# One PSUM layout for the spectral part and the attention loop, and the first scores between the last spectral products

## The chip, the core and the metric

The kernel runs on one core of a Trainium2 chip. The core has a matrix engine (TensorE, PE in the profile; its weight loads are shown apart as PEld), VectorE (DVE), ScalarE (ACT), GpSimd (POOL) and the DMA queues, the main one of which is issued from SyncE (SP). TensorE writes its results to PSUM, which here is used as eight banks of 128 x 512 float32 values. VectorE and ScalarE read PSUM; GpSimd works only on SBUF in this kernel. The metric is device time in microseconds of one execution; lower is better.

## What is computed

The input is x with 2048 rows of 512 values. The output mixes full multi-head attention (32 heads of 16 values) with a Fourier mixing layer, by a gate for each row:

```python
qkv = (x @ wqkv)                                   # 2048 x 1536
q, k, v = split_heads(qkv)                         # 32 heads of 16
p = softmax(einsum("qd,kd->qk", q, k) / 4)         # 2048 x 2048 for each head
a = concat_heads(p @ v) @ wo
re, im = x_b @ dft_hid_re.T, x_b @ dft_hid_im.T    # 2048 x 512
b = dft_seq_re @ re - dft_seq_im @ im              # the spectral part
g = sigmoid((x * gate_w).sum(-1))
out = g * a + (1 - g) * b
```

All is float32. The kernel feeds TensorE with pairs (hi, lo) of rounded values where it needs the precision: a product of two matrices is then three products, hi x hi, hi x lo and lo x hi.

## The kernel before, in words

The softmax subtracts a maximum for each query, so the kernel first *scans*: TensorE computes scores with queries on the partitions, and VectorE takes their maximum. The maxima then enter the real scores as two more rows of the operands (`m_d`, the hi and lo of the negated maximum), so that ScalarE can evacuate a score tile with one exponential. A scan is one pair of matmuls, for two heads at once; there are 1024 of them (`TOTAL`), of which the first 692 (`FRONT`) are put between the matmuls of the earlier parts, and the rest into the attention loop.

The parts stand in this order:

1. Projections of q, k, v, and the hidden transform of the spectral part (lines 317 to 526).
2. The spectral products (lines 528 to 604): 96 units `n` of a coefficient block (`coef`), four units (u = 0 to 3) to an output tile of 128 rows `t`. A unit covers four of the 16 sequence blocks `s`. Each block is three products, each product two matmuls that use one half of the rows of TensorE each (`halves_of`). The output tile lies in one two-bank PSUM tile, `xy`, of which there are two that take turns. `beside()` after each product puts a folded scan in where its pace says so: such a scan uses one of four single banks, d0, d1, k0, k1; ScalarE evacuates one half of the keys (`fold`, line 153) and VectorE folds the other half into it with the maximum (line 155). `prepare` (line 307) has GpSimd split the coefficients of unit n + 3 into hi and lo, in two rings of four tiles. A finished tile is evacuated in two halves, `tx` on ScalarE (line 598) and, for the last tile, `ty` on VectorE (line 600).
3. The attention loop (lines 893 to 936): 512 steps, for 16 pairs of heads p, two halves h of the queries and 16 blocks kb of keys. A step computes the scores of two heads and two query groups c of 512. Group c = 0 goes to a two-bank tile (`bank2`, the tag s3) and one wide exponential into `eb` (line 649); group c = 1 goes to two single banks (`bank`, the tag s2, three of them) and two narrow exponentials into `e` (line 653), the second one (j = 1) first. Between the two groups stands a scan (`next_scan`, line 130) in another two-bank tile (`pair_banks`, the tag s1). At the end of a step the sums of the step before are added up in `pvb` (`pv`, line 660): four column groups of TensorE, one for each head and query group. Step 0 has no sums. From step 333 (`MIX`) on the last spectral tiles and the output projection fill the place of the scans.

The order of the work is the order in which the source issues it (`manual_schedule`); every engine runs its own instructions in that order, and semaphores hold an instruction until its operands are there and its tile is free. Before, the PSUM pools of the spectral part (`psf`, `psk`) end before the pool of the loop (`ps2`) begins, so the first tiles of the loop take over banks from tiles of other names and shapes.

Of the kernel before, what the change touches and what calls it, by code (L numbers as in the profile page):

```python
# [25 lines left out]
ND = D // P  # L26
NC = S // 512
VC = DH + 1
SCALE = DH ** -0.5
# [6 lines left out]
FRONT = 564 + 16 * LATER  # L36
# [5 lines left out]
MIX = TOTAL - FRONT + 1  # L42
OUT = MIX + NB * LATER
SLOW = 3


def build(tc, x, xT, wqkv, wo, wrT, wiT, cr, ci, gate, out):
    nc = tc.nc
    with ExitStack() as ctx:
        keep = ctx.enter_context(tc.tile_pool(name="keep", bufs=1))  # L50
        stk = ctx.enter_context(tc.tile_pool(name="stk", bufs=6))
        sm = ctx.enter_context(tc.tile_pool(name="sm", bufs=2))
        big = ctx.enter_context(tc.tile_pool(name="big", bufs=1, reuse_waits="tile"))
        dram = ctx.enter_context(tc.tile_pool(name="dram", bufs=1, space=DRAM))

        q_d = [dram.tile([P, 2, S], F32, name=f"q_d{f}") for f in range(ND)]
        k_d = [dram.tile([P, 2, S], F32, name=f"k_d{f}") for f in range(ND)]
# [24 lines left out]
        scanned, used, unfolded = {}, {}, {}  # L82
# [99 lines left out]
        def block(i):  # L182
            return big.tile([P, 512], F32R, tag=f"b{i}", name=f"b{i}")

        ah, al = {}, {}


        seen, slots, due, count = [0], [0], [], [0]
        pace = [None, 0.0]
        with ExitStack() as pf:  # L190
            psf = pf.enter_context(tc.tile_pool(name="psf", bufs=2, space=PSUM))
            cw = pf.enter_context(tc.tile_pool(name="cw", bufs=4, reuse_waits="tile"))

            def s1():
                return pss1[0].tile([P, 2, 512], F32, tag="s1", name="s1")
# [56 lines left out]
            beds = []  # L252
# [41 lines left out]
            coef = []  # L294
# [4 lines left out]
            coef = coef[:len(coef) - NU * LATER]  # L299
# [7 lines left out]
            def prepare(n, copy=nc.gpsimd.tensor_copy, sub=nc.gpsimd.tensor_sub):  # L307
                if n >= len(coef):
                    return
                hi, lo = (cw.tile([P, 512], F32R, tag=tag, name=tag + "_").rearrange("p (c q) -> p c q", q=P)  # L310
                          for tag in ("chi", "clo"))
                raw = craw.pop(n)
                copy(hi, raw)
                sub(lo, raw, hi.bitcast(F32))
                ready[n] = hi, lo

            with ExitStack() as px:
# [11 lines left out]

                def new_cw():  # L330

                    return [[cw.tile([P, 512], F32R, tag=tag, name=tag + "_") for d in range(ND)]
                            for tag in ("chi", "clo")]

                def split_w(w, d, raw, engine=nc.vector, cols=slice(0, 512)):
                    split(w[0][d][:, cols], w[1][d][:, cols], raw[:, cols], engine)
# [188 lines left out]
                    project_s(wi, t, -1.0, use)  # L525
                run_due(True)

            with ExitStack() as py:
# [5 lines left out]
                psk = py.enter_context(tc.tile_pool(name="psk", bufs=1, space=PSUM, reuse_waits="tile"))  # L534
                beds += [lambda tag: psk.tile([P, 512], F32, tag=tag, name="s"), cp]
                for n in range(4, 8):
                    fetch(n)
                for d in range(4):
# [3 lines left out]
                pss, yre, early = {}, {}, {}  # L542
# [8 lines left out]
                for n, (ph, t, u) in enumerate(coef):  # L551
# [11 lines left out]
                    hi, lo = ready.pop(n)  # L563
# [21 lines left out]
                    for w in range(CS):  # L585
                        s = u * CS + w
                        for i, (c_, a_) in enumerate(((hi, ah[s]), (hi, al[s]), (lo, ah[s]))):
                            halves_of(pss[t], c_[:, w, :], a_, s == 0 and i == 0, s == NB - 1 and i == 2)
                            beside()
                        if swap:  # L590
                            if s == 7:
                                for i in range(8, 11):
                                    early[i] = load_operand(1, i, cp)
                            after(1 + 3 * (s % 8), renew, s)
                    if u == NU - 1:
                        tx = cp.tile([P, D], F32, tag="tx", name="tx")
                        ty = cp.tile([P, D], F32, tag="ty", name="ty")
                        nc.scalar.mul(tx, pss[t][0], gm[:, t:t + 1])
                        if n == len(coef) - 1:
                            nc.vector.tensor_scalar_mul(ty, pss[t][1], gm[:, t:t + 1])  # L600
# [5 lines left out]
        assert seen[0] == FRONT, seen[0]  # L606

        with ExitStack() as pa:
            ps2 = pa.enter_context(tc.tile_pool(name="ps2", bufs=1, space=PSUM, reuse_waits="tile"))
# [4 lines left out]
            pvb = ps2.tile([P, 512], F32, tag="pv", name="pvb")  # L614
            nc.vector.memset(pvb, 0.0)
            rb = ap.tile([P, 512], F32, name="rb")
            nc.gpsimd.memset(rb, 1.0)


            both = [pr.tile([P, 2, 512], F32, name=f"eb{i}") for i in range(4)]  # L620
            single = [[pr.tile([P, 512], F32, name=f"e{j}_{i}") for i in range(3 + j)] for j in range(2)]
            turn = [0, 0]

            def pair_banks():
                return ps2.tile([P, 2, 512], F32, tag="s1", name="s1")

            def bank():
                return ps2.tile([P, 512], F32, tag="s2", name="s2", bufs=3)

            def bank2():  # L630
                ps = ps2.tile([P, 2, 512], F32, tag="s3", name="s3")
                return ps, (ps[:, 0, :], ps[:, 1, :])

            def qk2(p, h, kb, c):
                n = turn[c]
                turn[c] += 1
                q0 = h * 1024 + c * 512
                qs, ks = used[p]
                if c == 0:
                    ps, pss = bank2()  # L640
                else:
                    pss = [bank() for j in range(2)]
                for j in range(2):
                    b = 64 * j
                    nc.tensor.matmul(pss[j], ks[b:b + 50, kb * P:(kb + 1) * P],  # L645
                                     qs[b:b + 50, q0:q0 + 512], start=True, stop=True)
                if c == 0:
                    e = both[n % len(both)]
                    nc.scalar.activation(e, ps, AF.Exp, scale=SCALE)  # L649
                    return [e[:, j, :] for j in range(2)]  # L650
# [5 lines left out]
            quads = [(c, j, 64 * c + 32 * j) for c in range(2) for j in range(2)]  # L656

            def pv(p, h, kb, es):
                for c, j, r in quads:
                    nc.tensor.matmul(pvb[r:r + VC, :], va[:, kb, 2 * p + j, :], es[c][j],  # L660
                                     start=kb == 0, stop=kb == NB - 1, tile_position=(0, r))

            def quotients(p, h):
                ob = ap.tile([P, 512], F32, tag="ob", name="ob", bufs=2)
# [193 lines left out]
            groups = {}  # L858

            def part(t, *ks):  # L860

                if t not in groups:
                    if t in (3, 8):
                        ps = pair_banks()
                        groups[t] = ps[:, 0, :], ps[:, 1, :]
                    else:
                        groups[t] = bank2()[1] if t == 9 else (bank(), pvb if t == 11 else bank())
                for k in ks:
                    mix_rest(t, groups[t], k, k == 0 or 7 < t < 11, k == 2)

# [22 lines left out]
            for step in range(NP * PERIODS):  # L893
                p, i = step // PERIODS, step % PERIODS
# [14 lines left out]
                        load_y(c + 2 * (step > OUT))  # L909
                if step >= MIX and step % 2 == 0:  # L910
                    next(fill)
                es = [qk2(p, h, kb, 0)]
                if step == 0:
                    es.append(qk2(p, h, kb, 1))
                if late:
                    late.pop(0)()
                next_scan()
                if step:
                    es.append(qk2(p, h, kb, 1))
                if step >= MIX and step % 2:  # L920
                    next(fill)
# [87 lines left out]
```

## Time and profile before

| | us |
|---|---|
| median of 3 runs | 1755.81 (1754.96 to 1759.93) |
| the profiled execution | 1751.4 |
| its span | 1749.6 |
| TensorE busy in the span | 1719.9 |
| ScalarE busy | 1451.9 |
| VectorE busy | 1155.1 |
| GpSimd busy | 712.7 |

The page adds up busy time over the whole span. Matmuls overlap, so a busy TensorE is not one at its peak. Times within the span are counted from its start. In the chain of work that ended last, each row is a stretch of one engine and line with its start and length; "issue" is time in which nothing that the profile shows was waited for. In the timeline a row gives start, length, engine, line, operation and tiles, and in brackets the idle time before it with what ended it. In a table by stretch a row gives the stretch, its length, the busy time (and count) of PE, PEld, DVE, ACT and POOL, then the clock granted to TensorE as a share of the full one, the share of the DMA engines and GB/s.

### The profile page before, as it was taken

What the parts mean: (1) busy time and instruction counts of PE and PEld (TensorE: products, weight loads), DVE (VectorE), ACT (ScalarE), POOL (GpSimd) and SP (SyncE); (2) the same over time, 40 slices, a digit from 0 to 9 for tenths busy, and PEclk for the clock granted to TensorE, in tenths of its full rate; (3) what the DMA queues carried; (4) which work ended last, traced back from release to release, by engine and by line L of the source; (5) the groups of instructions that cost most, each with busy time, mean ns of one, the idle gap of its engine ahead of it and who ended that gap; (6) DMA issues with size and microseconds to landing.
All of it is one profiled execution on the core that took longest, in us unless ns stands there. A gap on an engine that the chain in (4) does not pass through costs nothing.

```text
span 1749.6 us, 35589 instructions
## 1 busy us (share of the span) xinstructions
PE 1719.9 (98%) x13640; PEld 1021.8 (58%) x13640; DVE 1155.1 (66%) x1876; ACT 1451.9 (83%) x2384; POOL 712.7 (41%) x814
## 2 busy tenths in 40 slices
PE   8999999999999999999999999999999999999998
PEld 6887787888888887333333333333334555555554
DVE  6799999999999887666666666666664212222333
ACT  5445346888887887999999999999999888888885
POOL 3678667555556664032322323232232322322222
PEclk9999999999999999999999999999999999999999
DMA  8782666434354445433232423515313254255612
GB/s 296 254 298 79 190 201 206 121 115 117 104 154 140 139 133 120 74 59 63 58 67 56 82 40 64 95 23 99 78 35 73 64 118 90 68 141 137 177 36 100
DMA packets 126810, 199.55 MB, mean 114 GB/s; under 512 B 54016, under 2 KB 56560, under 8 KB 119728
## 3 DMA queue, kind: packets, MB, share of 16 engines
q1 hardware_dynamic: 84368, 161.02, 34.4%
q0 software_dynamic: 38496, 19.47, 5.2%
q10 hardware_dynamic: 3776, 16.78, 3.6%
q8 instruction: 107, 1.75, 0.4%
q14 instruction: 63, 0.52, 0.1%
HBM read 133.04 MB, written 63.71 MB: 112 GB/s over the span
## 4 chain that ended last, share of the span: by engine, by line
PE 89%; DMA 3%; DVE 3%; POOL 2%; issue 2%; ACT 1%; SPq 0%; DVEq 0%; ACTq 0%; POOLq 0%
PE pvb L660 28%; PE xy L180 21%; PE s L645 19%; PE s L180 8%; PE s L149 7%; PE s L130 6%; DVE mx L132 1%; DMA fa<-ks_d 1%; DMA kf_d<-fa 1%; POOL s L215 1%; DMA raws<-wqkv 0%; DMA raws<-xT 0%; POOL el L215 0%; POOL fa L215 0%; DMA abr<-ab_d 0%
## 5 line engine op out<-in xcount | busy, mean ns | idle before, releaser
L132 DVE TENSOR_REDUCE mx<-s 128x2 f32<-128x1024 f32 x524 | 627.2, 1222 | 207.5 <-PE s L130 207.4
L649 ACT ACTIVATE eb<-s 128x1024 f32<-128x1024 f32 x512 | 579.3, 1131 | 55.1 <-PE s L645 55.1
L653 ACT ACTIVATE e<-s 128x512 f32<-128x512 f32 x1024 | 610.3, 708 | 0.4 <-PE s L645 0.4
L660 PE MATMUL pvb<-e,va 128*17 128x512 f32 x2048 | 517.3, 598 | 0.0
L660 PE MATMUL pvb<-eb,va 128*17 128x512 f32 x2048 | 517.1, 598 | 0.0
L645 PE MATMUL s<-qs,ks 50*128 50x512 f32 x2048 | 428.1, 438 | 2.3 <-DVE ty L600 1.6
L645 PEld LDWEIGHTS s<-qs,ks 50*128 50x128 f32 x2048 | 212.6, 185 | 372.4 <-ACT eb L649 282.6
L155 DVE CUSTOM_DVE_ANT_0 fold<-s,fold 128x512 f32<-128x512 f32 x500 | 339.1, 690 | 39.0 <-PE s L149 19.4
L153 ACT ACTIVATE fold<-s 128x512 f32<-128x512 f32 x500 | 296.1, 602 | 70.0 <-PE s L149 43.1
L149 PE MATMUL s<-ks,qs 48*128 48x512 f32 x1000 | 223.3, 404 | 7.6 <-DVE mx L155 6.1
L130 PE MATMUL s<-ks,qs 48*128 48x512 f32 x1048 | 221.6, 396 | 3.7 <-DVE mx L132 2.5
L668 POOL DMA_DIRECT2D lc<-ob x124 | 63.1, 515 | 308.2 <-DVE ob L665 307.9
L660 PEld LDWEIGHTS pvb<-eb,va 128*17 128x17 f32 x2048 | 69.2, 96 | 190.2 <-issue 182.0
L149 PEld LDWEIGHTS s<-ks,qs 48*128 48x128 f32 x1000 | 120.9, 184 | 47.6 <-DVE mx L155 18.2
L675 POOL DMA_DIRECT2D r_d<-lc x31 | 18.1, 585 | 294.9 <-DVE lc L674 286.0
L130 PEld LDWEIGHTS s<-ks,qs 48*128 48x128 f32 x1048 | 108.3, 184 | 14.9 <-DVE mx L132 6.0
L180 PE MATMUL xy<-w,b 64*128 64x512 f32 x768 | 105.2, 392 | 0.2 <-ACT s L379 0.2
L401 ACT ACTIVATE tx<-xy 128x512 f32<-128x512 f32 x48 | 28.7, 599 | 78.6 <-PE xy L180 52.5
L754 DVE SCALAR_TENSOR_TENSOR y<-s,g,y 128x512 f32<-128x512 f32 x50 | 36.6, 748 | 76.6 <-PE s L180 76.0
L677 POOL DMA_DIRECT2D rb<-r_d x124 | 60.6, 496 | 63.0 <-DMA r_d<-lc 63.0
L180 PE MATMUL s<-b,chi 64*128 64x512 f32 x542 | 85.2, 390 | 0.3 <-ACT chi L963 0.3
L180 PEld LDWEIGHTS xy<-w,b 64*128 64x128 f32 x768 | 72.5, 186 | 17.6 <-ACT s L379 1.0
(750 smaller groups left out, 2320.4 us busy)
## 6 DMA issues: line engine op xcount, KB each, us to landing
craw<-ci SPq DMA_DIRECT2D x64, 256.0 KB
craw<-cr SPq DMA_DIRECT2D x60, 256.0 KB
ks<-k_d SPq DMA_DIRECT2D x46, 256.0 KB
qs<-q_d SPq DMA_DIRECT2D x46, 256.0 KB
ab_d<-ab SPq DMA_DIRECT2D x32, 256.0 KB
y_d<-y SPq DMA_DIRECT2D x32, 256.0 KB
o_d<-oh POOLq DMA_DIRECT2D x28, 256.0 KB, 9.8
o_d<-ol POOLq DMA_DIRECT2D x28, 256.0 KB, 11.9
```

The source lines that it names most:

```text
L130: nc.tensor.matmul(ps[:, j, :], qs[b:b + 48, qb * P:(qb + 1) * P], ks[b:b + 48, c * 512:(c + 1) * 512], start=True, stop=True)
L132: nc.vector.tensor_reduce(mx[p][:, :, qb, c], ps, axis=AX.X, op=ALU.max)
L149: nc.tensor.matmul(ps, qs[b:b + 48, qb * P:(qb + 1) * P], ks[b:b + 48, c * 512:(c + 1) * 512], start=True, stop=True)
L153: nc.scalar.activation(fold[j], ps, AF.Relu)
L155: nc.vector.tensor_tensor_reduce(out=fold[j], in0=ps, in1=fold[j], scale=1.0, scalar=-3.0e38, op0=ALU.add, op1=ALU.max, accum_out=mx[p][:, ...
L180: nc.tensor.matmul(ps[j], lhs[r], rhs[r], start=first, stop=last)
L645: nc.tensor.matmul(pss[j], ks[b:b + 50, kb * P:(kb + 1) * P], qs[b:b + 50, q0:q0 + 512], start=True, stop=True)
L649: nc.scalar.activation(e, ps, AF.Exp, scale=SCALE)
L653: nc.scalar.activation(e[j], pss[j], AF.Exp, scale=SCALE)
L660: nc.tensor.matmul(pvb[r:r + VC, :], va[:, kb, 2 * p + j, :], es[c][j], start=kb == 0, stop=kb == NB - 1, tile_position=(0, r))
L668: nc.gpsimd.dma_start(lc[32 * n:32 * n + 32, :], ob[r + DH:r + VC, :].rearrange("p (s e) -> p s e", e=16))
L677: nc.gpsimd.dma_start(rb[r:r + DH, :], r_d[p][h][n:n + 1, :].to_broadcast([DH, 512]))
```

## The change

1. *PSUM.* One pool, `psf`, now holds two two-bank tiles, `wide0` and `wide1`, for the whole kernel, and `psk` the four single banks d0, d1, k0, k1 from the spectral part on. In the spectral part the two wide tiles take turns as `xy`; in the loop `wide0` serves the scans (s1) and `wide1` the first scores (s3); d0, d1, k0 are the single banks of the second scores, taken in the order of their last use (`order_`), and k1 holds the sums `pvb`.
2. *The first scores.* `qk_both` computes one score pair into `wide1` with its exponential. It is called three times in the last two units of the last spectral tile of part 2, behind the blocks s = 9, 11 and 14: both query groups of step 0 (both by a wide tile and a wide exponential now), and the first group of step 1. `pvb` is cleared at the first call.
3. *The loop's start.* Step 0 issues nothing but the note that its exponentials exist (`continue`), so it has no scan either; step 1 begins with the sums of step 0 and then issues its second group only. All later scans stand one step later.
4. *SBUF.* The hi and lo of a coefficient block lie in one tile of 128 x 2 x 512 of a ring of four (`ring4`); the wide exponentials `eb` take over the same ring. The last `ty` uses another ring's tile.

```diff
+SCANS_IN = 0
+AHEAD = (9, 11, 14)
...
+        ring4 = ctx.enter_context(tc.tile_pool(name="ring4", bufs=4, reuse_waits="tile"))
+        psf = ctx.enter_context(tc.tile_pool(name="psf", bufs=1, space=PSUM, reuse_waits="tile"))
...
+        def wide(i, name):
+            return psf.tile([P, 2, 512], F32, tag=f"wide{i}", name=name)
+
+        def coefficients():
+            t = ring4.tile([P, 2, 512], F32R, tag="c", name="c")
+            return t[:, 0, :], t[:, 1, :]
...
+        def qk_both(p, h, kb, c=0):
+            ps = wide(1 - SCANS_IN, "s3")
+            qk(p, h, kb, c, [ps[:, j, :] for j in range(2)])
+            if len(both) < 4:
+                both.append(ring4.tile([P, 2, 512], F32, tag="c", name="eb"))
+            e = both[ebs[0] % 4]
+            ebs[0] += 1
+            nc.scalar.activation(e, ps, AF.Exp, scale=SCALE)
+            return [e[:, j, :] for j in range(2)]
...
             def xy():
-                ps = psf.tile([P, 2, 512], F32, tag="xy", name="xy")
+                turns[0] += 1
+                ps = wide(turns[0] % 2, "xy")
...
+            order_ = ["d0", "d1", "k0"]
+
+            def bank():
+                order_.append(order_.pop(0))
+                return narrow(order_[-1], "s2")
...
+                        if n >= len(coef) - 2 and s in AHEAD:
+                            if not ahead:
+                                sums.append(narrow("k1", "pvb"))
+                                nc.vector.memset(sums[0], 0.0)
+                            ahead.append(qk_both(0, 0, int(s == AHEAD[2]), int(s == AHEAD[1])))
...
             def pair_banks():
-                return ps2.tile([P, 2, 512], F32, tag="s1", name="s1")
+                return wide(SCANS_IN, "s1")
...
                 for j in (1, 0):
                     nc.scalar.activation(e[j], pss[j], AF.Exp, scale=SCALE)
+                order_[-2:] = order_[-1], order_[-2]
                 return e
...
-                es = [qk2(p, h, kb, 0)]
                 if step == 0:
+                    pend.append((p, h, kb, ahead[:2]))
+                    continue
+                if step == 1:
+                    flush()
+                es = ahead[2:] if step == 1 else [qk2(p, h, kb, 0)]
+                if step == 1:
                     es.append(qk2(p, h, kb, 1))
                 if late:
                     late.pop(0)()
                 next_scan()
-                if step:
+                if step > 1:
                     es.append(qk2(p, h, kb, 1))
```

More of the change, by code (lines that the diff above doesn't have):

```diff
@@ L183, in block, with qk @@
             return big.tile([P, 512], F32R, tag=f"b{i}", name=f"b{i}")
-        ah, al = {}, {}
+        turns = [0]
+        def wide(i, name):
[3 more added lines that the diff above has]
+            return t[:, 0, :], t[:, 1, :]
+        ah, al = {}, {}
+        quads = [(c, j, 64 * c + 32 * j) for c in range(2) for j in range(2)]
+        both = []
+        def qk(p, h, kb, c, pss):
+            q0 = h * 1024 + c * 512
+            qs, ks = used[p]
+            for j in range(2):
+                b = 64 * j
+                nc.tensor.matmul(pss[j], ks[b:b + 50, kb * P:(kb + 1) * P],
+                                 qs[b:b + 50, q0:q0 + 512], start=True, stop=True)
+        def qk_both(p, h, kb, c=0):
[7 more added lines that the diff above has]
+            return [e[:, j, :] for j in range(2)]
+        ebs, ahead, sums = [0], [], []
         seen, slots, due, count = [0], [0], [], [0]
@@ L190, in build @@
         with ExitStack() as pf:
-            psf = pf.enter_context(tc.tile_pool(name="psf", bufs=2, space=PSUM))
-            cw = pf.enter_context(tc.tile_pool(name="cw", bufs=4, reuse_waits="tile"))
             def s1():
@@ L309, in prepare @@
                     return
-                hi, lo = (cw.tile([P, 512], F32R, tag=tag, name=tag + "_").rearrange("p (c q) -> p c q", q=P)
-                          for tag in ("chi", "clo"))
+                hi, lo = (t.rearrange("p (c q) -> p c q", q=P) for t in coefficients())
                 raw = craw.pop(n)
@@ L330, in new_cw @@
                 def new_cw():
-                    return [[cw.tile([P, 512], F32R, tag=tag, name=tag + "_") for d in range(ND)]
-                            for tag in ("chi", "clo")]
+                    return list(zip(*(coefficients() for d in range(ND))))
                 def split_w(w, d, raw, engine=nc.vector, cols=slice(0, 512)):
@@ L526, in build, with narrow @@
                 run_due(True)
+            psk = ctx.enter_context(tc.tile_pool(name="psk", bufs=1, space=PSUM, reuse_waits="tile"))
+            def narrow(tag, name):
+                return psk.tile([P, 512], F32, tag=tag, name=name)
+            order_ = ["d0", "d1", "k0"]
+            def bank():
+                order_.append(order_.pop(0))
+                return narrow(order_[-1], "s2")
             with ExitStack() as py:
@@ L532, in fetch @@
                         load_coef(n, cp.tile([P, CS, P], F32, tag="craw", name="craw", bufs=5))
-                psk = py.enter_context(tc.tile_pool(name="psk", bufs=1, space=PSUM, reuse_waits="tile"))
-                beds += [lambda tag: psk.tile([P, 512], F32, tag=tag, name="s"), cp]
+                beds += [lambda tag: narrow(tag, "s"), cp]
                 for n in range(4, 8):
@@ L594, in build @@
                             after(1 + 3 * (s % 8), renew, s)
+                        if n >= len(coef) - 2 and s in AHEAD:
+                            if not ahead:
+                                assert seen[0] == FRONT, (seen, n, s, pace)
+                                sums.append(narrow("k1", "pvb"))
+                                nc.vector.memset(sums[0], 0.0)
+                            ahead.append(qk_both(0, 0, int(s == AHEAD[2]), int(s == AHEAD[1])))
                     if u == NU - 1:
                         tx = cp.tile([P, D], F32, tag="tx", name="tx")
-                        ty = cp.tile([P, D], F32, tag="ty", name="ty")
+                        last = n == len(coef) - 1
+                        ty = cp.tile([P, D], F32, tag="raw" if last else "ty", name="ty", bufs=3 if last else 2)
                         nc.scalar.mul(tx, pss[t][0], gm[:, t:t + 1])
-                        if n == len(coef) - 1:
+                        if last:
                             nc.vector.tensor_scalar_mul(ty, pss[t][1], gm[:, t:t + 1])
@@ L604, in build @@
                 run_due(True)
-        assert seen[0] == FRONT, seen[0]
+        assert seen[0] == FRONT and turns[0] % 2 == SCANS_IN, (seen, turns)
         with ExitStack() as pa:
-            ps2 = pa.enter_context(tc.tile_pool(name="ps2", bufs=1, space=PSUM, reuse_waits="tile"))
             pr = pa.enter_context(tc.tile_pool(name="pr", bufs=1, reuse_waits="tile"))
@@ L612, in build @@
             ap = pa.enter_context(tc.tile_pool(name="ap", bufs=1, reuse_waits="tile"))
-            pvb = ps2.tile([P, 512], F32, tag="pv", name="pvb")
-            nc.vector.memset(pvb, 0.0)
+            pvb = sums[0]
             rb = ap.tile([P, 512], F32, name="rb")
             nc.gpsimd.memset(rb, 1.0)
-            both = [pr.tile([P, 2, 512], F32, name=f"eb{i}") for i in range(4)]
             single = [[pr.tile([P, 512], F32, name=f"e{j}_{i}") for i in range(3 + j)] for j in range(2)]
-            turn = [0, 0]
+            turn1 = [0]
             def pair_banks():
-                return ps2.tile([P, 2, 512], F32, tag="s1", name="s1")
[L627 to L632, printed above, removed]
+                return wide(SCANS_IN, "s1")
             def qk2(p, h, kb, c):
[L635 to L638, printed above, removed]
                 if c == 0:
[L640 to L650, printed above, removed]
+                    return qk_both(p, h, kb)
+                n = turn1[0]
+                turn1[0] += 1
+                pss = [bank() for j in range(2)]
+                qk(p, h, kb, c, pss)
                 e = [ring[n % len(ring)] for ring in single]
@@ L653, in qk2 @@
                     nc.scalar.activation(e[j], pss[j], AF.Exp, scale=SCALE)
+                order_[-2:] = order_[-1], order_[-2]
                 return e
-            quads = [(c, j, 64 * c + 32 * j) for c in range(2) for j in range(2)]
             def pv(p, h, kb, es):
@@ L661, in pv, with bank2 @@
                                      start=kb == 0, stop=kb == NB - 1, tile_position=(0, r))
+            def bank2():
+                ps = wide(1 - SCANS_IN, "s3")
+                return ps[:, 0, :], ps[:, 1, :]
             def quotients(p, h):
@@ L866, in part @@
                     else:
-                        groups[t] = bank2()[1] if t == 9 else (bank(), pvb if t == 11 else bank())
+                        groups[t] = bank2() if t == 9 else (bank(), pvb if t == 11 else bank())
                 for k in ks:
```

## The prediction

> **What bounds the kernel now.** I read the page first (span, busy time, chain by engine), then the chain in order of time around the place that the change touches, then the timeline there, and last tables by stretch for the clock.
>
> ```profile
> span 1749.6 us, 35589 instructions
> PE 1719.9 (98%) x13640; PEld 1021.8 (58%) x13640; DVE 1155.1 (66%) x1876; ACT 1451.9 (83%) x2384; POOL 712.7 (41%) x814
> PE 89%; DMA 3%; DVE 3%; POOL 2%; issue 2%; ACT 1%; SPq 0%; DVEq 0%; ACTq 0%; POOLq 0%
> ```
>
> TensorE is busy for 98% of the span and carries 89% of the chain. Time can only be won where TensorE waits or runs slowly. The change touches one such place, the seam between the last spectral product and the attention loop. This is the chain there:
>
> ```profile
> 688.55 0.50 PE s L149
> 689.05 4.35 PE xy L180 x36
> ...
> 693.48 0.70 ACT tx L598
> ...
> 694.20 0.76 DVE ty L600
> ...
> 695.01 0.69 PE s L645 x2
> ...
> 695.78 1.03 ACT eb L649
> ...
> 696.85 0.80 PE s L645 x2
> 697.65 0.61 PE s L130 x2
> 698.26 0.43 PE s L645 x2
> 698.69 1.84 PE pvb L660 x8
> ...
> 703.45 0.43 PE s L645 x2
> 703.88 0.23 PE s L130 x2
> 704.11 0.23 PE s L645 x2
> 704.34 0.98 PE pvb L660 x8
> 705.33 0.43 PE s L645 x2
> ```
>
> The spectral products end at 693.40 (689.05 + 4.35). The first scores wait for both evacuations of the last spectral tile (tx on ScalarE, then ty on VectorE), the second scores wait for the first exponential, and the sums (pvb) of step 0 take 1.84 us where 0.98 is normal later. Step 3 is the first step at the steady pace: it starts at 703.45, and the next one at 705.33, 1.88 us later. So the seam lasts 703.45 - 693.40 = 10.05 us, for three steps of which the first has no sums.
>
> Why 1.84 and not 0.98? Tables by stretch (the busy time of TensorE comes second, the granted clock after the count of POOL):
>
> ```profile
> 545.81:549.22 3.41, 1.81 (x15) 1.32 (x14) 3.41 (x8) 0.97 (x3) 1.23 (x1) 1.00 0.26 78
> 549.22:552.63 3.41, 3.41 (x18) 2.98 (x17) 2.22 (x7) 1.95 (x5) 0.85 (x2) 0.50 0.04 9
> 569.71:573.11 3.40, 1.91 (x17) 1.59 (x18) 1.72 (x5) 2.60 (x5) 1.28 (x1) 1.00 0.78 241
> 573.12:576.53 3.41, 3.41 (x32) 2.75 (x32) 2.70 (x9) 2.30 (x5) 1.91 (x2) 1.00 0.11 40
> 692.58:695.99 3.41, 1.79 (x13) 1.04 (x9) 1.24 (x2) 0.90 (x2) 0.96 (x1) 1.00 0.00 0
> 695.99:702.82 6.83, 6.13 (x25) 1.93 (x28) 3.55 (x3) 5.33 (x9) 2.06 (x3) 0.50 0.64 151
> 702.82:712.00 9.18, 9.18 (x74) 3.29 (x70) 5.37 (x6) 8.55 (x14) 0.00 (x0) 1.00 0.56 89
> ```
>
> The clock was halved from 549.22 to 552.63 and from 695.99 to 702.82: lengths of 3.41 and 6.83 (twice 3.41), and the two starts lie 146.77 = 43 x 3.413 apart. So in this trace the clock is decided on a grid of 3.41 us. It fell after cells in which TensorE was busy for 1.81 and 1.79 us, and stayed after a cell with 1.91. A cell must be idle for about 1.6 us (3.41 - 1.81) to lose the clock; the seam's first gap alone (693.40 to 695.01) does that, if one cell holds it.
>
> The Trainium skill ("TensorE: Matmul & The Clock Gate", Part 1) calls the window free-running, 3413 ns long, which the grid of 3.41 agrees with. It also asks for a whole idle window before the clock falls, and under "Why this matters for your kernels" only forbids gaps above some 3 us; by that rule the seam would cost no clock, before or after. Here the trace disagrees: 1.6 us of idle time was enough, twice.
>
> **The change, part by part.** In the order of the built programs, TensorE has the same instructions in number; SP's and POOL's queues keep their order throughout. Differences stand at the seam alone, and one wide exponential replaces two narrow ones.
>
> *Three score pairs between the last spectral products.* They come after blocks 9, 11 and 14 of the last accumulation, the first right behind the last folded scan (688.55). A pair that finds its operands costs 0.23 (row 704.11), so 3 x 0.23 = 0.69, and the spectral part ends at 694.09. Do they wait? Their loads must have landed, their two banks must be free, and ScalarE must keep up:
>
> ```profile
> 688.39 0.60 ACT L153 ACTIVATE fold<-s 128x512 f32<-128x512 f32 x1 [0.17 <-PE s L149]
> 688.00:690.00 2.00, 1.81 (x16) 1.23 (x14) 1.84 (x6) 0.82 (x2) 0.00 (x0) 1.00 0.04 11
> 690.00:693.40 3.40, 3.38 (x29) 2.50 (x26) 0.00 (x0) 0.00 (x0) 0.00 (x0) 1.00 0.00 0
> 705.26 0.50 PE L645 MATMUL s<-qs,ks 50*128 50x512 f32 x2
> 705.80 1.04 ACT L649 ACTIVATE eb<-s 128x1024 f32<-128x1024 f32 x1
> ```
>
> ScalarE's last fold ends at 688.99, and from 690.00 to 693.40 ScalarE, VectorE and the DMA engines do nothing: the exponentials have a free engine. The loads are all there by 690.00 at the latest (the DMA share before that is 0.04), so pair 1 could wait 1.0 at most. An exponential starts 0.54 after its pair (705.26 to 705.80) and takes 1.03. Pair 1 at about 689.0 gives its banks back at 690.6; six products (1.4 us) lie before pair 2, at 690.65, so it waits for next to nothing. Pair 3 stands nine products (2.1 us) behind that. I take no wait; the bound above is 1.03 for each of the two.
>
> *The two waits that go.* The scores no longer wait for ty (1.61) nor step 1's for step 0's exponential. TensorE goes from the products straight into the sums of step 0 (0.98, to 695.07) and the second scores of step 1 (0.43 after sums, to 695.50). The memset of pvb now stands on VectorE before ty, behind its last fold, in the idle stretch above: nothing.
>
> *What is late next: ty again.* The first scan of the loop writes the banks of the last spectral tile, so it waits for ty, with tx now queued behind the third exponential. Pair 3 starts at 693.17 (its end, 693.40, is 694.09 less the last three products, 0.69); exponential 693.71 to 694.74; tx 0.70 and ty 0.76 with 0.02 between each: 696.24; scan at 696.28. TensorE idles 0.78 from 695.50. Then step 2's scan waits for the first scan's reduction:
>
> ```profile
> 703.72 0.39 PE L130 MATMUL s<-ks,qs 48*128 48x512 f32 x2
> 704.16 1.23 DVE L132 TENSOR_REDUCE mx<-s 128x2 f32<-128x1024 f32 x1 [1.21 <-PE s L130]
> ```
>
> The reduction begins 0.44 after its scan: 696.28 + 0.44 + 1.23 + 0.04 = 697.99, and the work between (two pairs, 0.46) leaves about 1.0 idle. Queued behind that scan are step 2's second scores and step 1's sums: 697.99 + 0.23 + 0.23 + 0.98 = 699.43 for the start of step 3, against 703.45. Gain 4.02.
>
> *One scan fewer at the seam.* Step 0 no longer scans, so every later scan stands one step later and the last falls into step 332, which had none:
>
> ```profile
> 1328.12 0.88 PE L645 MATMUL s<-qs,ks 50*128 50x512 f32 x4
> 1329.97 0.93 PE L645 MATMUL s<-qs,ks 50*128 50x512 f32 x4
> ```
>
> Without its scan that step took 1.85 against 1.88 with one (705.33 - 703.45): ScalarE fills it. So the scan costs about 0.03 there; the bound above is its whole 0.23. The next block of spectral work reuses those banks, but a step later, behind the reduction.
>
> *One layout of PSUM, single banks by last use.* In the loop each second score still waits for the first of the two exponentials of the step before, as the built program of before has it; every other wait of the steady loop is the same too. Nothing, with a bound in the rivals. *hi and lo in one tile.* POOL's split of a coefficient now waits for the last product with either half, one or two products later (0.23 to 0.46):
>
> ```profile
> 677.70 0.61 POOL L313 CAST chi__10814<-craw 128x512 fp32r<-128x512 f32 x1 [1.98 <-PE xy L180]
> 678.39 1.30 POOL L314 TENSOR_TENSOR clo__10815<-craw,chi__10814 128x512 fp32r<-128x512 f32 x1
> 690.27 0.39 PE L180 MATMUL xy<-b,chi__10814 64*128 64x512 f32 x1
> ```
>
> Split by 679.69, used at 690.27: 10.6 us of cover. If POOL fell that far behind, its 1.9 us for each coefficient would show; I take nothing.
>
> **Sum.** -4.02 + 0.03 = -4.0 us. The profiled execution took 1751.4 (span 1749.6), which gives 1747.4. The median of the runs shown is 1755.81, 4.4 above the profiled one; the same gain from it gives 1751.8, my forecast. 0.3% of this kernel, 5.3 us, is about what a measurement tells from no change, so this is a real gain below that bound.
>
> **The rivals.**
>
> *The clock falls again.* Both new gaps (0.8 and 1.0) lie between 695.5 and 698.0. A cell that holds 1.6 of their 1.8 us loses the clock as the two cells above did. The grid lies by chance in each run: of 3.41 us of positions about 1.3 do it, 4 in 10. A cell at half clock costs half of 3.41, 1.7: 1753.5. By the skill's rule of a whole idle window this could not happen; I go by the rows.
>
> *More than 0.3% faster.* The runs behind the median are 4.4 slower than the profile. If that is partly one more cell of half clock at the seam, 1.7, the change takes it too: -5.7, 1750.1. If the loop's first scans also found no wait (0.78 + 1.0 less), -5.8, 1750.0. Against it: the reduction's 1.23 is a hard row, and the profile shows only its own two cells.
>
> *Slower, by the loop's banks.* ScalarE is as full as TensorE in the loop:
>
> ```profile
> 900.00:1100.00 200.00, 200.00 (x1480) 76.07 (x1474) 135.69 (x127) 200.00 (x318) 63.04 (x93) 1.00 0.33 63
> ```
>
> If the new banks made a step's second scores wait for the later exponential, or the new places of the tiles slowed ScalarE, no slack would hide it. It decides from 9.3 us (4.0 + 5.3), 18 ns on each of 511 steps; 30 ns gives 1767. For it: 200.00 of 200.00. Against it: the loop's waits are unchanged.
>
> *Nothing happens.* Pairs 2 and 3 wait about 1.0 each for ScalarE, and the clock falls as before: -4.0 + 2.0 + 1.7 leaves 1755.5.
>
> **How the numbers follow.** Forecast 0.40, clock 0.24, more than 0.3% faster 0.18, slower 0.10, nothing 0.08. The forecast's own range is 1750 to 1753.5 (its waits up or down by 1.8); about 0.08 of its chance lies below 1750.5 (1755.81 less 5.3). So faster 0.18 + 0.08 = 0.26, same 0.32 + 0.24 + 0.08 = 0.64, slower 0.10. The range goes from 1748.9, the fast rival less the 1 us by which the lower two runs differ, to 1757, which takes in the clock rival and the case of nothing with some of the scatter upward; it leaves out the slow rival and a little below.
>
> **What would show it.** Right: the products end about 0.7 later, followed at once by sums; the first scan waits for ty, the second for the reduction; step 3 starts some 6 us after 693.4; no clock row of 0.50 near 696; steps of 1.88 after that. Wrong: score pairs that wait for ScalarE between the products, a half clock from 697 to 700, steps longer than 1.88, or a longer step 332.

## The result and the profile after

| | before, us | after, us |
|---|---|---|
| median of 14 runs each, taken in turns | 1756.05 | 1749.86 |
| the profiled execution | 1751.4 | 1749.47 |
| its span | 1749.6 | 1747.7 |

The ratio of the times is 0.9969, with a 95% interval from 0.996 to 0.9979: 5.4 us less, between 3.7 and 7.0 (the two medians lie 6.2 apart). The forecast was 4.0 less, and 1751.8. The median of before moves by some microseconds from one chip or hour to the next (1756.05, 1752.95 and 1754.96 in the three sessions told of here), so below each kernel is compared with the runs of before in its own session.

The profiled execution gained only 1.9, less than the runs. Where that went stands under experiment 5. The page of the kernel after, its head and the chain by engine:

```profile
span 1747.7 us, 35504 instructions
PE 1717.2 (98%) x13640; PEld 1020.7 (58%) x13640; DVE 1154.7 (66%) x1876; ACT 1451.8 (83%) x2383; POOL 712.4 (41%) x814
PE 86%; DMA 5%; DVE 3%; POOL 2%; issue 2%; ACT 1%; SPq 0%; DVEq 0%; POOLq 0%; ACTq 0%
```

TensorE has the same number of instructions and is busy for 2.7 us less; ScalarE has one instruction less. Now the seam, as the chain of waits of the kernel after has it (start, length, what):

```profile
688.32 0.49 PE s L153
688.81 0.24 PE xy L184 x2
689.05 0.23 PE s L209 x2
689.28 1.39 PE xy L184 x10
690.67 0.29 PE s L209 x2
690.96 2.08 PE xy L184 x18
693.04 0.25 PE s L209 x2
...
693.37 0.66 ACT eb L220
...
694.29 0.69 ACT tx L652
...
695.01 0.76 DVE ty L654
...
695.81 0.52 PE s L134 x2
...
696.36 1.24 DVE mx L136
...
697.63 0.49 PE s L134 x2
698.13 0.24 PE s L209 x2
698.37 0.98 PE pvb L693 x8
699.35 0.43 PE s L209 x2
...
701.23 0.43 PE s L209 x2
```

The three score pairs (L209) stand between the products (L184). The third exponential, tx and ty follow one another; the first scan of the loop (695.81) waits for ty, the second (697.63) for the reduction of the first. The sums take 0.98. Step 3 starts at 699.35 and step 4 1.88 later. Counted from the last folded scan, the last thing that both kernels do alike, step 3 comes after 699.35 - 688.32 = 11.03 us, where before it came after 703.45 - 688.55 = 14.90: the seam is 3.87 shorter.

The timeline of the kernel after (in brackets the idle time before, and what ended it):

```profile
690.46 0.19 PEld L209 LDWEIGHTS s<-qs,ks 50*128 50x128 f32 x2 [0.22 <-ACT eb L220]
693.37 1.02 ACT L220 ACTIVATE eb<-s 128x1024 f32<-128x1024 f32 x1 [1.28 <-PE s L209]
695.81 0.50 PE L134 MATMUL s<-ks,qs 48*128 48x512 f32 x2 [0.42 <-DVE ty L654]
697.63 0.49 PE L134 MATMUL s<-ks,qs 48*128 48x512 f32 x2 [1.09 <-DVE mx L136]
```

TensorE idles 0.42 and 1.09 there. Tables by stretch of the kernel after, on the grid of its clock (each stretch of 3.41 us is called a cell; the second number is TensorE's busy time, the one behind POOL the granted clock):

```profile
690.52:693.93 3.41, 3.41 (x33) 2.52 (x34) 0.00 (x0) 1.58 (x2) 0.00 (x0) 1.00 0.00 0
693.93:697.34 3.41, 2.19 (x16) 0.59 (x14) 1.74 (x2) 2.83 (x5) 1.42 (x2) 1.00 0.00 0
697.34:700.75 3.41, 3.12 (x26) 1.10 (x26) 2.16 (x3) 2.28 (x4) 1.59 (x2) 1.00 0.35 103
```

The cell that holds most of both gaps was busy for 2.19 and the clock stayed. So in this execution the change does what it says and the half clock at the seam is gone.

### The profile page after: what moved, and what is told of

It is laid out like the page before. It is cut to its first block, busy times and chain, and to the rows that moved or that the text cites. A ratio compares the mean times of both kernels' runs of the same rounds, so it can differ in the third digit from the quotient of the medians.

```text
span 1747.7 us, 35504 instructions
## 1 busy us (share of the span) xinstructions
PE 1717.2 (98%) x13640; PEld 1020.7 (58%) x13640; DVE 1154.7 (66%) x1876; ACT 1451.8 (83%) x2383; POOL 712.4 (41%) x814
## 4 chain that ended last, share of the span: by engine, by line
PE 86%; DMA 5%; DVE 3%; POOL 2%; issue 2%; ACT 1%; SPq 0%; DVEq 0%; POOLq 0%; ACTq 0%
PE pvb L693 27%; PE xy L184 21%; PE s L209 18%; PE s L184 8%; PE s L153 7%; PE s L134 6%; DMA lc<-ob 2%; DVE mx L136 2%; DMA fa<-ks_d 1%; DMA kf_d<-fa 1%; POOL s L252 1%; DMA raws<-xT 1%; DMA raws<-wqkv 0%; POOL el L252 0%; POOL fa L252 0%
## 5 line engine op out<-in xcount | busy, mean ns | idle before, releaser
L209 PE MATMUL s<-qs,ks 50*128 50x512 f32 x2048 | 427.2, 436 | 0.0
L209 PEld LDWEIGHTS s<-qs,ks 50*128 50x128 f32 x2048 | 210.2, 184 | 367.8 <-ACT eb L220 279.1
L184 PE MATMUL xy<-b,c 64*128 64x512 f32 x2640 | 418.4, 393 | 0.3 <-ACT c L318 0.3
L184 PEld LDWEIGHTS xy<-b,c 64*128 64x128 f32 x2640 | 296.7, 187 | 19.9 <-ACT c L318 0.6
L350 POOL TENSOR_TENSOR c<-craw,c 128x512 fp32r<-128x512 f32 x92 | 120.0, 1304 | 7.4
L349 POOL CAST c<-craw 128x512 fp32r<-128x512 f32 x92 | 56.3, 612 | 141.2 <-PE xy L184 137.3
L184 PE MATMUL xy<-w,b 64*128 64x512 f32 x768 | 105.2, 392 | 0.2 <-ACT s L414 0.2
```

The costliest lines, as they stand in the source:

```text
L184: nc.tensor.matmul(ps[j], lhs[r], rhs[r], start=first, stop=last)
```

## The experiments

The first four tell apart what the seam's gain is made of (the layout, the inserted scores, the clock) and what the order of the banks is worth. The last four ask where the profiled execution lost time again, and how regular the seam is. The two groups ran on two chips. "Seam" is always the time from the last folded scan to the start of step 3, read from the chain as above; "half" means that the trace shows a granted clock of 0.50 for 6.83 us there.

| kernel | seam | half | median (runs) | ratio to before, 95% interval |
|---|---|---|---|---|
| before | 14.90 | yes | | |
| after | 11.03 | no | 1749.86 (14) | 0.9969 (0.996 to 0.9979) |
| 1 layout alone | 14.70 | yes | 1751.25 (12) | 0.9984 (0.9973 to 0.9996) |
| 2 two pairs ahead | 10.60 | no | 1748.11 (12) | 0.997 (0.9956 to 0.9984) |
| 3 before, with filling | 12.55 | no | 1751.89 (12) | 0.9991 (0.9979 to 1.0003) |
| 4 plain rotation | 11.06 | no | 1817.06 (1) | |
| 5 after, division later | 12.38 | yes | 1748.34 (6) | 0.9961 (0.9946 to 0.9976) |
| 5b before, division later | 15.41 | yes | 1753.7 (12) | 0.9993 (0.9976 to 1.0009) |
| 6 as 2, division later | 10.56 | no | 1746.6 (7) | 0.9959 (0.9944 to 0.9974) |
| 7 after, once more | 11.08 | no | 1748.93 (9) | 0.9962 (0.9949 to 0.9975) |

### 1. The layout alone

```diff
-AHEAD = (9, 11, 14)
+AHEAD = ()
```

The first steps of the loop are issued as before; only the one PSUM layout is left of the change.

> The new PSUM layout and tiles as in the changed kernel, but no scores between the spectral products: step 0 issues its own scores and its scan again. Theory A (the gain is the seam, and the layout alone opens most of it, because the first scores no longer share banks with the last spectral tile and so don't wait for its evacuation): step 3 starts about 3.2 us earlier after the last products than before (3.9 in the changed kernel), by waits worked out from before's rows: scan at 695.0 for ty, next scan at 696.8 for the first reduction, step 3 at 700.2 instead of 703.4; median -3 where the clock stays, -1.5 where it falls. Theory B (the scores between the products are the gain): no difference to before, within 1 us. Theory C (the gain lies in the loop's steady steps, by the bank order): as fast as the changed kernel, about -5.5, with steps shorter than 1.88.

The trace gives a seam only 0.2 shorter, as theory B has it, and not the 3.2 of theory A. Its chain of waits:

```profile
694.03 0.76 DVE ty L654
694.79 0.09 issue
694.89 0.48 DVE pvb L668
695.37 0.00 issue
695.37 1.24 DVE mx L136
...
697.87 1.84 PE pvb L694 x8
...
701.29 1.78 PE pvb L694 x8
```

Two things eat the gain. The memset of pvb stands between ty and the first reduction on VectorE, on the path for 0.48; in the changed kernel it runs at 689.84 beside the products. And the clock fell at 696.06, so that the sums take 1.84 and 1.78. By the ratio the runs are 2.8 faster than before's (0.7 to 4.7), more than this trace shows. Its runs had a mean granted clock of 0.9966 against 0.9953 for before in the same session; of a span of 1750 the difference is 2.3 us. That agrees with a seam at which the clock falls in some runs only, but also with cells lost less often elsewhere; the trace of one run can't show which.

### 2. Two pairs ahead in place of three

```diff
-AHEAD = (9, 11, 14)
+AHEAD = (9, 11)
...
-                es = ahead[2:] if step == 1 else [qk2(p, h, kb, 0)]
+                es = [qk2(p, h, kb, 0)]
```

> Only step 0's two score pairs stand between the products; step 1 issues its own first scores behind the sums of step 0. ScalarE can then evacuate the last spectral tile right behind the products instead of behind a third exponential. Theory A (the seam's end is set by the chain products, tx, ty, first scan, reduction, second scan): the first scan comes about 1 us earlier, step 3 about 1.0 us earlier than in the changed kernel, median 1 us below it (-6.4 to before). Theory B (scores ahead are what pays, the more of them the better): slower than the changed kernel by the third pair's share, about +0.5 to +1.

Timeline of this kernel:

```profile
693.39 0.69 ACT L652 ACTIVATE tx<-xy,gm 128x512 f32<-128x512 f32 x1 [1.75 <-PE xy L184]
695.88 0.50 PE L209 MATMUL s<-qs,ks 50*128 50x512 f32 x2 [0.46 <-ACT eb L220]
696.75 0.49 PE L134 MATMUL s<-ks,qs 48*128 48x512 f32 x2 [0.37 <-DVE mx L136]
```

Without the third exponential tx starts as soon as the products end, ty is done when the first scan wants its banks, and the idle times are 0.46 and 0.37 in place of 0.42 and 1.09. The seam is 0.43 shorter than after's. The third pair therefore costs 0.43 rather than gaining: half of what was expected, but in the expected direction. Experiment 6 shows the same against 7 (10.56 and 11.08). By their medians the two can't be told apart from the changed kernel.

### 3. The clock alone

```diff
+                        if n == len(coef) - 1:
+                            idle = [beds[0](tag) for tag in ("k0", "k1")]
+                            for _ in range(6):
+                                halves_of(idle, hi[:, CS - 1, :], ah[NB - 1], True, True)
```

The kernel before, with six products that nobody reads behind the last unit; they fill the gap in which the clock fell.

> The kernel before, with six more product pairs behind the last spectral product, into two banks that nobody reads: TensorE works through the wait for ty, which itself stays (the products are extra work that no result uses). Theory A (about 2.9 us of the seam's 10.05 are the half clock, the rest waits): the clock row near 696 shows 1.00, the sums of step 0 take 0.98 instead of 1.84, step 3 starts some 2.5 to 2.9 us earlier than before; median -2 to -2.9. Theory B (the waits alone are the loss, the clock costs little): no difference to before, within 0.5 us.

In the chain of waits of this kernel the old order stands, at the full clock:

```profile
695.19 0.91 PE s L649 x4
696.09 0.25 PE s L130 x2
...
697.65 0.50 PE s L130 x2
698.15 0.24 PE s L649 x2
698.39 0.98 PE pvb L664 x8
...
701.26 0.44 PE s L649 x2
```

Step 3 starts at 701.26, 12.55 behind the last folded scan: 2.35 less than before, a little under the 2.5 to 2.9 expected. In the traces, holding the clock is thus worth 2.35 of the 3.87 by itself; the remaining 1.5, the difference between this seam and after's at the same full clock, is the work that the gaps now hold. The runs don't confirm it: by the ratio they are 1.6 faster, with an interval that includes nothing. This trace lost 2.9 again in the loop, to waits of the kind that experiment 5 is about.

### 4. Plain rotation of the single banks

```diff
                 for j in (1, 0):
                     nc.scalar.activation(e[j], pss[j], AF.Exp, scale=SCALE)
-                order_[-2:] = order_[-1], order_[-2]
                 return e
```

> The changed kernel with the single banks taken in plain rotation: without the swap after the two narrow exponentials, the second score of each step takes the bank that the later exponential of the step before reads. Theory A (the order by last use is what keeps the loop at 1.88): a step cannot end before that exponential, which ends 2.68 after its step's start; with 0.57 from a step's start to its second scores that gives about 2.15 for a step, +0.27 on each of the first 330 steps and less on those after: +90 to +140 us. Theory B (the order of the banks doesn't matter, other waits cover it): the changed kernel's time within 3 us.

1817.06 in the one run, with a span of 1815.3 against 1747.7: 67.6 longer. Groups of instructions of this kernel and of the kernel after in the same stretch, from 900 to 1100 us (count, busy time, mean ns, idle time before and its releasers):

```profile
L687 ACT ACTIVATE e<-s 128x512 f32<-128x512 f32 x201 | 108.8, 599 | 0.0
L209 PEld LDWEIGHTS s<-qs,ks 50*128 50x128 f32 x400 | 55.4, 184 | 95.8 <-ACT eb L220 64.6 <-ACT e L687 21.4
```

```profile
L687 ACT ACTIVATE e<-s 128x512 f32<-128x512 f32 x211 | 128.5, 733 | 0.0
L209 PEld LDWEIGHTS s<-qs,ks 50*128 50x128 f32 x420 | 42.9, 184 | 89.4 <-ACT eb L220 88.5 <-ACT e L687 0.8
```

The scores now wait for the narrow exponentials (21.4 in place of 0.8), and 200 us hold 201 of these in place of 211, so a step takes 1.99 in place of 1.90. With two of three banks taken a step and given back in the order (1, 0), one score of the next step gets the bank that the step before gives back last. On average a step loses 0.10 up to step 332 and 0.20 behind step 342: 69 from step 3 to the last, below the expected 90 to 140. The swap of two names is worth more than ten times what the whole change gains; the changed layout couldn't do without it.

### 5. The division later, in both kernels

The profiled execution of the kernel after is 4.0 ahead at step 3 and still 4.0 ahead at step 92, but 3.5 at step 112, 3.1 at step 172 and 2.3 at step 252. Three single steps lost it: 106, 170 and 234, by 0.57, 0.57 and 1.00. The timeline around the last one, and the DMA issues there (KB each, us to landing):

```profile
1122.23 2.03 POOL L705 DMA_DIRECT2D lc<-ob  x4 [7.21 <-DVE ob L702]
1136.20 0.25 DVE L711 RECIPROCAL lc<-lc 128x16 f32<-128x16 f32 x1 [1.81 <-DMA lc<-ob]
```

```profile
lc<-ob POOLq DMA_DIRECT2D x4, 2.0 KB, 12.5
```

Once in each half of a head pair the four row sums are gathered by four small DMAs of GpSimd, and VectorE divides by them seven steps after the half's last sums, 12.1 us behind the issue. Here the DMAs had landed only 13.8 behind it. VectorE stood for 1.81, the next reduction came late, and TensorE's scan waited for it from 1136.64 to 1137.59. The diff doesn't touch this. To see whether it explains the loss, the division was put two steps later:

```diff
-                    halved.append((step + (7 if done[0] < NP - 1 else 3), quotients(*done[:2])))
+                    halved.append((step + (9 if step < MIX else 7 if done[0] < NP - 1 else 3), quotients(*done[:2])))
```

> The changed kernel with the division of a half's sums due 9 steps after its last sums instead of 7, up to step 332. In the traces so far the reciprocal stands on VectorE 12.1 us behind the issue of the four small transfers that it needs, and these land 11 to 14 us behind it wherever ten loads of the next pair are issued at the same time; where they land later than 12.1, VectorE stands still, the next scan's reduction with it, and TensorE up to 1 us. Theory D (these stalls, 0 to 3 us in a run, are the part of the difference between runs that the seam does not explain): no reciprocal waits over 0.1 us before step 332, no steps of 2.4 to 3.1 us, median 1 to 2 us below the changed kernel and less scatter. Theory E (the stalls are absorbed by the step's slack, or move elsewhere): the changed kernel's time within 0.5 us.

> The kernel before with the same later division and nothing else. Theory D: 0.5 to 2 us below the kernel before; the difference to the changed kernel with the later division is then the seam alone, 3.9 us where the clock falls at the seam (all of 6.8 us at half clock) and less where it falls for a shorter time. Theory E: the time of the kernel before within 0.5 us.

The gaps of TensorE over 0.6 us before step 333 that followed such a wait are gone from the trace of the changed kernel with this edit. But the medians move by 0.6 and 1.3 only (1748.34 against 1748.93 for after, 1753.7 against 1754.96 for before), which the scatter of the runs doesn't tell from nothing. So what these waits cost in a usual run isn't shown, and neither is theory D or E. The two kernels with the edit differ by 5.4, more than the 3.9 that theory D gave to the seam. In before's trace the longest such wait ahead of step 333 was 0.8 us, and the loop of kernels 1 and 2, which have after's banks, took 1026.59 from step 3 to the last, as before's did (1026.58), against 1028.69 for after. Experiment 3, with before's banks, lost more still to the same waits (1029.51). So the loss in after's profile doesn't come from the layout: with either layout there are traces with it and without. One thing spoke against the remedy: with the division later the DMAs landed up to 16.7 behind their issue, and one wait of 1.0 was left. Why they landed later isn't settled.

The trace of this kernel brought something else, at a seam with the same instructions as after's:

```profile
692.46:695.87 3.41, 2.03 (x14) 0.48 (x6) 1.89 (x2) 2.82 (x5) 1.58 (x2) 1.00 0.00 0
695.87:702.70 6.83, 6.69 (x28) 1.93 (x30) 2.53 (x3) 3.27 (x6) 1.43 (x2) 0.50 0.78 164
```

```profile
697.23 1.84 PE pvb L693 x8
699.07 0.72 PE s L209 x2
...
702.48 0.55 PE s L209
...
703.51 0.98 PE pvb L693 x8
```

Its clock fell, for two cells. Step 3 starts 12.38 behind the last folded scan (686.69), and step 3 itself takes 3.41. Step 4 therefore starts 15.79 behind it, against 701.23 - 688.32 = 12.91 in the kernel after: the fall costs 2.9 by then and 3.0 by step 5. Where it happens, only 0.9 of the seam's gain is left.

### 6. Two pairs ahead and the division later

> Only step 0's two pairs between the products, and the later division: both gains together. By the looks so far the seam is 0.45 us shorter than in the changed kernel (11.12 against 11.57 from the last folded scan to step 3's first exponential) and its two gaps, 0.46 and 0.37, are too short for the clock to fall; with theory D 1.5 to 2.5 us below the changed kernel, and the fastest of all. With theory E 0.5 below it.

The edits of 2 and 5 together. The lowest median of all, 1746.6 (0.9959), but its interval and those of 5 and 7 cover one another; nothing says that it beats the changed kernel. One late division was left in its trace (landed 17.8 behind the issue, TensorE's gap 1.08).

### 7. The changed kernel once more

> The changed kernel itself, beside the others on the same chip. Theory A: 3.5 to 5.5 us below the kernel before; its look shows the seam at 11.6 us from the last folded scan to step 3's first exponential and full clock there, whatever the grid, because its two gaps together (0.42 and 1.09) are less than the 1.6 us of idle time that the cells that lost the clock had. Rival (the clock falls there in 4 runs of 10): a cell of 0.50 between 697 and 700.

The seam is 11.08, and the clock stayed: 2.66 and 2.64 busy in the two cells that share the gaps. Waits of the division for its DMAs, of 1.2, 0.5, 2.5 and 0.6, are there again. But the same seam in experiment 5 did lose its clock, so the theory that the gaps are harmless wherever the grid lies falls. By the ratio the gain is 6.7 (4.4 to 9.0), above the 3.5 to 5.5 expected.

## Why the prediction was right, and where its steps were off

The forecast of 1751.8 lies 1.9 above the measured median, within its own range of 1750 to 1753.5 but for 0.1, and the gain of 4.0 lies in the measured interval of 3.7 to 7.0. The mechanism is the one foretold, but some of the agreement is luck. Of four traces with after's seam one lost its clock, and there only 0.9 of the gain was left. The profiled execution itself took 1749.5, not the 1747.4 that the sum gives: the seam gained what was said, and the division's late DMAs, which the prediction doesn't mention, took most of the 2.1 back that the loop lost.

- *The seam's gain*, forecast 4.02: 3.87 from the last folded scan. Right, and by the chain that was foretold: products, third exponential, tx, ty, first scan, reduction, second scan. The 0.15 between them is made of three terms: the first scan came 0.24 earlier than forecast, its reduction began 0.55 behind it instead of 0.44, and the second scan, which starts out of a gap, took 0.49 where 0.23 was put.
- *The pairs find their operands.* Each took 0.23 to 0.29. Pair 1 came 0.73 behind the start of the last folded scan, one product later than forecast (0.45). The weight load of pair 2 waited 0.22 for the first exponential, where next to nothing was forecast; products were still running, so the chain has no gap there.
- *The gaps*, forecast 0.78 for ty and about 1.0 for the reduction: 0.42 and 1.09. Counted from the last folded scan, the first scan came at 7.49 instead of 7.73, because tx started at 5.97 instead of 6.21, and TensorE's work before it ended at 7.07 instead of 6.95. Both shrank the first wait; the second one grew a little.
- *The scan moved into step 332*, forecast 0.03: the kernel after is 2.2 ahead of before on both sides of that step, so the step costs too little to read. Right.
- *The clock.* Rival "the clock falls again" had 4 in 10 and 1.7. It happened in one of the four traces with after's seam (experiment 5, not in after, 4 or 7), in the cell that held 1.38 of the two gaps' 1.51. Its price was mis-sized: the fall lasted two cells and cost 3.0 in place of 1.7. Why two isn't shown. Idle time in the first halved cell doesn't explain it: in 5b that cell was busy for all its 3.41 and the clock still stayed away for another, while the halved cell of experiment 3 at 569.87 held 0.16 of idle time and was the only one. With that price it would have ended near 1755, hardly to be told from no change.
- *The rule of 1.6 us idle.* Added up cell by cell over ten traces, up to 1730 us: of the cells at full clock, all seven in which TensorE was busy for less than 1.66 us were followed by a halved clock, of 17 with 1.67 to 1.86 seven were, and above that only one, that of experiment 5 with 2.03. So the 1.8 was a fair reading of where the clock is lost, about half of a cell, but as a band and not as an edge. The cell that breaks it contains a scan, sums and two gaps; the sums use 17 columns of the array. That they count less is a guess, and after's cell of 2.19 with the same sums stayed. It is open.
- *The loop's banks.* No steady wait changed, as forecast. The rival's mechanism is real, though: experiment 4 has it, at 0.10 to 0.20 a step, much above the 18 ns from which it decides.
- *More than 0.3% faster.* The measured 5.4 is 0.31%, on the edge of that case. Its reason, one more half cell at the seam than the profile shows, isn't shown: three traces with the old seam (before, 1, 5b) all have the two cells. What the runs show is the mean granted clock. It was 0.9953 and 0.9950 for before (29 and 21 runs) and 0.9976 and 0.9978 for after (14 and 9). The two cells at the seam are 6.83 / 2 of a span of 1750, 0.0020; so even if every run of before lost them and none of after, the difference of 0.0023 to 0.0028 would be a little more than they give. Some of it must be scatter or come from elsewhere in the kernel; where isn't shown. What is left of the time beside the clock fits the traces: in the session of experiment 7 the mean times differ by 6.3, of which the clock's difference makes 4.8, and the other 1.5 is what the seams of 3 and after differ by at full clock. The excess of 1.4 over the forecast is inside the interval; whether anything more than scatter stands behind it stays open.

The Trainium skill ("TensorE: Matmul & The Clock Gate", Part 1) lets the clock fall after at least one idle window of some 3.4 us. These runs keep the grid and contradict the condition: 14 cells lost the clock with 0.6 to 1.85 us of work in them, and none of the seams here has a whole idle cell. By that condition of the Trainium skill experiment 3 could have gained nothing at the seam; it gained 2.35.

## What to carry to other kernels

Where a busy engine has a seam with two or three short gaps, look at the granted clock across it before costing the gaps: here, in the traces, 2.35 of the seam's gain of 3.87 came from a clock that stayed, and products that nobody reads were enough to hold it, though the runs of that kernel don't show a gain clear of their scatter. Work put ahead must not queue in front of what the seam still waits for: the third score pair delayed the evacuation by its exponential and cost 0.43. And when buffers of one pool serve a loop, take them in the order in which they were last read; a rotation by name alone cost 68 us here, in the one run of it.

## What the runs showed of the hardware that was not expected

The four DMAs of 2 KB from GpSimd's queue had all landed 3.1 to 5.7 us behind the first one's issue in quiet places of the loop, and 10.6 to 13.8 where SyncE issued 7 to 15 other transfers, of up to 256 KB, beside them (first 19 of these groups in the trace after). A single one took 1.5 to 5.0 from its own issue (median 2.9) in the quiet groups and 6.3 to 12.7 (median 10.0) in the crowded ones. The Trainium skill ("DMA: Bandwidth & Descriptors", Anatomy of one DMA) puts such a transfer at about 2.0 us plus its bytes, an estimate of 2.0 here; the quiet median is about one and a half times that, the crowded one five times. A division that waits for such a DMA 12.1 behind its issue is on time by luck.

A clock lost once needn't return after one cell: at every seam that lost it, in before and in experiments 1, 5 and 5b, it stayed away for two cells (6.83), while elsewhere, as at 549.22 in before, it was back after one (3.41).
